# More repeated identity passes while TensorE waits for the last weights

## Chip, cores, metric

One core of a Trainium2 chip. The metric is the device time of one execution in microseconds (us); medians are quoted with their ranges. A profiled execution's span, from its first to its last recorded event, is some 1.8 us shorter than its time. "Clock" is the share of full speed that the throttle granted TensorE.

## The reference, cut to what matters

Sparse causal attention (8 batches, 8 heads, 576 positions, 64 per head) feeds a spectral mix. Each of the 64 lowest frequencies m is multiplied by its own complex 512 x 512 weights; those weights are nearly all of the data read.

```python
X = np.fft.rfft(x, axis=1)
Xr, Xi = (np.real(X[:, :n_modes]), np.imag(X[:, :n_modes]))
Yr = np.einsum('bmd,mde->bme', Xr, w_r) - np.einsum('bmd,mde->bme', Xi, w_i)
Yi = np.einsum('bmd,mde->bme', Xr, w_i) + np.einsum('bmd,mde->bme', Xi, w_r)
Y[:, :n_modes] = Yr + 1j * Yi
y = np.fft.irfft(Y, n=S, axis=1)
u = x + y
return (u + np.maximum(u @ w_ch, 0.0)).astype(np.float32)
```

## The kernel before

The weights come in two halves of 64 modes each. `mode` is 16 matmuls of 16 columns. After mode 53 of the second half TensorE has little left to do until weights land, and the kernel issues `again`: matmuls of 512 columns with the identity matrix, whose result nobody reads ("passes" below), to keep TensorE's clock up for what follows. Modes 60 to 63 have loads of their own; earlier modes share one in pairs.

```python
def mode(slot, m):
    ...                                   # cut: w_fetch, bank choice
    for e in range(4):
        for c in range(4):
            nc.tensor.matmul(yv[:, mi, e, :], wt[pr, XC[c], ds(128 * e, 128)],
                             Xh[half][pr, c, :, :, m],
                             start=(c == 0), stop=(c == 3))
    ...                                   # cut: after modes 61 and 63 VectorE adds into YT

def again(n):
    for i in range(n):
        nc.tensor.matmul(warm, idn, v0s[0][:, 2, :], start=True, stop=True)

warm = psum("v")
for m in range(END, NM):                  # 54 .. 63
    mode(1, m)
    if m < END + 2:
        for w in early[3 * (m - END) : 3 * (m - END) + 3]:
            w()                           # five matmuls of the output stage
    else:
        again(0 if m < NM - 6 else 4 if m < NM - 2 else 2)
spec_last(0)                              # four products, four transposes of YT
again(3)
v_early(2, warm)
spec_out(3, 0, *held[0])                  # ScalarE, VectorE: copies to zz and yy
for i in range(len(units)):               # output stage, 36 tiles
    v_rows(i)                             # cut; starts with a matmul on zz
    ...
```

The softmax here doesn't subtract the row's maximum and nothing guards it: scores larger than these inputs give would overflow.

## Time and profile before

| | kernel before |
|---|---|
| time, three runs | 434.84 us median (434.26 to 434.90) |
| profiled execution | span 433.8 us, so a time of 435.61 us |
| busy share PE, VectorE, ScalarE | 78%, 50%, 43% |
| chain that ended last | DMA 69%, PE 18% |
| granted clock, mean | 0.833 |

In TensorE's timelines L547 is `mode`, L951 `again`, L886 and L884 the last spectra, and L688 with v<-zz the first work of the output stage.

### The profile page before, as it was taken

To read this page: it belongs to the slowest core of one execution; us is meant where nothing else is said; L and a number is where in the kernel's file an instruction comes from. 1 tells how busy PE (TensorE), PEld (TensorE's weight loads), DVE (VectorE), ACT (ScalarE), POOL (GpSimd) and SP (SyncE) were. 2 spreads that over 40 slices of the span, in tenths; PEclk is the share of its full clock that TensorE was granted. 3 is DMA by queue.
4 is the path that set the end of the run, shared out by engine and by line. 5 is a ranking of instruction groups with operands and counts; after the bars stand their busy time and mean duration, and the time that the engine had idled before them with its cause. 6 is when DMAs were issued, how large, how long until landed. Compare 5 with 4: busy or idle time off the path is not lost.

```text
span 433.8 us, 12099 instructions
## 1 busy us (share of the span) xinstructions
PE 338.7 (78%) x5307; PEld 244.0 (56%) x5307; DVE 215.1 (50%) x466; ACT 188.1 (43%) x353; POOL 128.9 (30%) x208
## 2 busy tenths in 40 slices
PE   1986888779886887889794566698669698977994
PEld 1865776657764665667663344465446465643441
DVE  2888678744523243342511033455346366503895
ACT  1686678635543435445340401133115122602892
POOL 6522332323232222222222222222222221200983
PEclk9999899869967659676855559868798899988999
DMA  8999999999999999999999999999999999991687
GB/s 178 212 213 213 215 212 212 212 210 213 215 212 214 213 214 213 213 214 214 213 213 213 213 213 215 213 213 215 213 213 213 214 213 213 214 179 29 260 331 275
DMA packets 28996, 92.18 MB, mean 212 GB/s; under 512 B 4048, under 2 KB 5072, under 8 KB 28944
## 3 DMA queue, kind: packets, MB, share of 16 engines
q0 software_dynamic: 24704, 81.28, 94.3%
q1 hardware_dynamic: 3440, 9.46, 5.8%
q10 hardware_dynamic: 800, 0.67, 0.6%
q8 instruction: 42, 0.69, 0.6%
q14 instruction: 10, 0.08, 0.0%
HBM read 163.22 MB, written 9.44 MB: 398 GB/s over the span
## 4 chain that ended last, share of the span: by engine, by line
DMA 69%; PE 18%; DVE 6%; ACT 3%; issue 2%; POOL 1%; DVEq 0%; POOLq 0%
DMA wt<-in_moe_w_i_dram 51%; DMA wt<-in_moe_w_r_dram 8%; DMA ring<-in_q_dram 5%; DMA w_ch<-in_moe_w_ch_dram 5%; DVE xb L250 2%; DVE kz L292 2%; PE y L547 2%; PE v L688 2%; PE u L688 2%; PE v L894 2%; PE sc L514 1%; ACT X L260 1%; DVE rec L249 1%; PE tp L395 1%; PE sc L353 1%
## 5 line engine op out<-in xcount | busy, mean ns | idle before, releaser
L547 PE MATMUL y<-X,wt 128*128 128x16 f16 (+1 forms) x2048 | 82.8, 192 | 59.5 <-DMA wt<-in_moe_w_i_dram 58.1
L547 PEld LDWEIGHTS <-wt 128*128 128x128 f16 (+1 forms) x2048 | 73.1, 103 | 75.4 <-issue 68.3
L196 POOL DMA_DIRECT2D wt<-in_moe_w_r_dram x62 | 36.4, 587 | 139.2 <-PE y L547 66.0
L196 POOL DMA_DIRECT2D wt<-in_moe_w_i_dram x60 | 35.2, 587 | 73.0 <-DMA wt<-in_moe_w_i_dram 60.2
L654 ACT ACTIVATE v<-sc 128x512 f16<-128x512 f32 x32 | 19.1, 596 | 68.4 <-PE sc L645 68.3
L471 ACT ACTIVATE PL<-sc 128x480 f16<-128x480 f32 (+1 forms) x48 | 27.7, 579 | 47.6 <-PE sc L457 46.9
L645 PE MATMUL sc<-w_cp,xT 128*128 128x512 f16 (+1 forms) x160 | 47.4, 424 | 0.0
L655 DVE COPY xo<-tp 128x512 f16<-128x512 f16 x32 | 22.1, 692 | 36.7 <-PE tp L653 36.4
L250 DVE TENSOR_TENSOR xb<-av,rec 90x256 f16<-90x256 f32 (+2 forms) x80 | 36.0, 450 | 2.8
L249 DVE RECIPROCAL rec<-av 90x4 f32<-90x4 f32 (+2 forms) x80 | 14.7, 183 | 45.3 <-PE av L486 33.9
L402 DVE COPY qT<-tp 128x576 f16<-128x576 f16 x16 | 12.0, 758 | 40.1 <-PE tp L395 37.2
L260 ACT ACTIVATE v<-tp 128x640 f16<-128x640 f16 (+1 forms) x24 | 19.4, 807 | 24.0 <-PE tp L429 21.1
L395 PE MATMUL tp<-cI_s,ring 64*64 64x64 f16 x864 | 26.4, 211 | 1.6 <-issue 0.8
L360 ACT ACTIVATE PL<-sc 90x360 f16<-90x360 f32 (+1 forms) x48 | 22.7, 490 | 6.2 <-PE sc L353 5.3
L926 DVE TENSOR_TENSOR osb<-u,rl 128x512 f32<-128x512 f32 x36 | 23.6, 689 | 3.3 <-ACT rl L907 1.7
L395 PEld LDWEIGHTS <-ring 64*64 64x64 f16 x864 | 20.7, 123 | 6.8 <-issue 3.6
L441 PE MATMUL sc<-cMl_s,cI_s 128*128 128x480 f16 (+1 forms) x48 | 23.0, 478 | 1.6 <-ACT X L260 1.6
L909 POOL TENSOR_TENSOR rl<-rl,xo 128x512 f32<-128x512 f32 x16 | 18.3, 1155 | 18.9 <-ACT rl L907 18.6
L457 PE MATMUL sc<-qT,kz 128*128 128x160 f16 (+1 forms) x160 | 23.4, 275 | 0.5 <-issue 0.5
L457 PEld LDWEIGHTS <-kz 128*128 128x128 f16 x160 | 16.8, 119 | 10.8 <-issue 8.1
L907 ACT ACTIVATE rl<-v 128x512 f32<-128x512 f32 x36 | 20.4, 597 | 4.9 <-PE v L688 4.2
L285 PE MATMUL tp<-cI_s,ring 72*128 72x72 f16 x256 | 15.1, 206 | 9.5 <-DMA ring<-in_v_dram 8.0
(103 smaller groups left out, 655.5 us busy)
## 6 DMA issues: line engine op xcount, KB each, us to landing
wt<-in_moe_w_r_dram POOLq DMA_DIRECT2D x62, 512.0 KB, 18.9
wt<-in_moe_w_i_dram POOLq DMA_DIRECT2D x60, 512.0 KB, 19.4
out_dram<-osb SPq DMA_DIRECT2D x14, 512.0 KB, 2.7
ring<-in_v_dram POOLq DMA_DIRECT2D x8, 288.0 KB, 13.4
ring<-in_q_dram POOLq DMA_DIRECT2D x8, 288.0 KB, 13.6
ring<-in_k_dram POOLq DMA_DIRECT2D x8, 288.0 KB, 13.0
ring<-in_v_dram POOLq DMA_DIRECT2D x3, 512.0 KB, 15.1
ring<-in_q_dram POOLq DMA_DIRECT2D x3, 512.0 KB, 14.8
```

Of the source, the lines that this page charges most:

```text
L196: nc.gpsimd.dma_start(dst, rows)
L250: nc.vector.tensor_tensor(out=dst, in0=val.rearrange("p h (q c) -> p h c q", c=4), in1=rec[0:n, 0:pieces] .to_broadcast((n, pieces, 64)) . ...
L260: nc.scalar.activation(out=out, in_=in_, func=ACTF.Copy)
L360: nc.scalar.activation(out=PS[0:n, ds(POFF[t], 4 * n)], in_=scp[0:n, 0 : 4 * n], func=ACTF.Exp, scale=SCALE,)
L395: nc.tensor.transpose(tp[ds(64 * hp, 64), ds(64 * i, 64)], qn[ds(64 * hp, 64), ds(64 * (9 * g + i), 64)], idn[ds(64 * hp, 64), ds(64 * hp, ...
L441: nc.tensor.matmul(scp[:, 0 : n * times].rearrange("p (h x) -> p h x", h=times), idn, mask_rows("cMl", n, times), start=True, stop=False,)
L457: nc.tensor.matmul(scp[:, ds(col, n)], kzs[par][:, hp, ds(s0, 128)], qTs[par][:, ds(s0, n)], start=False, stop=(i == len(todo) - 1),)
L471: nc.scalar.activation(out=dst, in_=src, func=ACTF.Exp, scale=SCALE)
L547: nc.tensor.matmul(yv[:, mi, e, :], wt[pr, XC[c], ds(128 * e, 128)], Xh[half][pr, c, :, :, m], start=(c == 0), stop=(c == 3),)
L645: nc.tensor.matmul(vp[pr, :], xT[:, ch, cols], w_chs["cp"][:, ch, :], start=(ch == 0), stop=(ch == 3),)
L655: nc.vector.tensor_copy(out=xo[pr].rearrange("p (h q c) -> p h q c", h=2, c=4), in_=tp[pr, 0:512].rearrange("p (h c q) -> p h q c", h=2, c=4),
L926: nc.vector.tensor_tensor(out=osb[:, t % 2, :], in0=up, in1=rls[b, t][:, t % 2, :], op=AluOp.add)
```

## The change

Intent: hold TensorE at full clock through the last spectra. The number of passes before mode 62 rises from 16 to 24, and three instead of two stand before mode 63.

```diff
-            again(0 if m < NM - 6 else 4 if m < NM - 2 else 2)
+            again({NM - 1: 2, NM - 2: 3, NM - 3: 10}.get(m, 7 if m > NM - 6 else 0))
```

| passes after mode | 58 | 59 | 60 | 61 | 62 | 63 | sum |
|---|---|---|---|---|---|---|---|
| before | 4 | 4 | 4 | 4 | 2 | 2 | 20 |
| changed | 0 | 7 | 7 | 10 | 3 | 2 | 29 |

## The prediction

> **What bounds the kernel now.** I read the page first. Its chain that ended last is 69% DMA, most of it weights, and its line of granted clock shows TensorE below full speed in many slices. So until the last weights land the kernel runs at the pace of their transfer, and what TensorE does before then counts only if it makes TensorE late for them. Next I read the chain of waits piece by piece for the stretch in which the diff acts; columns are start, length, what.
>
> ```profile
> 364.40 19.38 DMA wt<-in_moe_w_i_dram
> ...
> 384.06 9.63 DMA wt<-in_moe_w_i_dram
> 393.83 0.64 PE y L547 x16
> 394.47 0.50 PE v L951 x2
> 394.97 1.77 PE y L886 x4
> 396.74 0.43 PE y L884 x4
> 397.17 1.18 PE v L951 x3
> 398.35 0.22 PE v L894
> 398.56 0.23 PE v L688
> ```
>
> From 384.06 to 393.69 the chain is a transfer, so the idle passes (L951) before it are off the path. From 393.83 TensorE's own pace is the path: mode 63, two passes, the four products and four transposes of the last spectra (L886, L884), three more passes, an early v, then the output stage. The same four L886 matmuls take 0.86 us later in this chain, at 408.68, against 1.77 here: the clock is at half speed here. The timeline of TensorE shows the sequence ahead of it:
>
> ```profile
> 383.92 0.64 PE L547 MATMUL y<-X,wt 128*128 128x16 f16 x16 [2.88 <-DMA wt<-in_moe_w_i_dram]
> 384.39 1.83 PE L951 MATMUL v<-v,cI_s 128*128 128x512 f16 x4
> 386.02 0.68 PE L547 MATMUL y<-X,wt 128*128 128x16 f16 x16
> 386.54 1.67 PE L951 MATMUL v<-v,cI_s 128*128 128x512 f16 x4
> 388.04 0.64 PE L547 MATMUL y<-X,wt 128*128 128x16 f16 x16
> 388.52 1.02 PE L951 MATMUL v<-v,cI_s 128*128 128x512 f16 x4
> 389.38 0.64 PE L547 MATMUL y<-X,wt 128*128 128x16 f16 x16
> 389.86 1.03 PE L951 MATMUL v<-v,cI_s 128*128 128x512 f16 x4
> 392.58 0.64 PE L547 MATMUL y<-X,wt 128*128 128x16 f16 x16 [1.69 <-DMA wt<-in_moe_w_i_dram]
> 393.83 0.64 PE L547 MATMUL y<-X,wt 128*128 128x16 f16 x16 [0.17 <-DMA wt<-in_moe_w_i_dram]
> ```
>
> These are modes 58 to 63 with their passes. Modes 62 and 63 wait for weights (1.69 and 0.17 us idle); 60 and 61 do not. The stretch table in half microseconds gives the clock (the last column but two):
>
> ```profile
> 387.50:388.00 0.50, 0.50 (x3) 0.15 (x1) 0.00 (x0) 0.00 (x0) 0.00 (x0) 0.63 0.54 107
> 394.50:395.00 0.50, 0.50 (x3) 0.13 (x2) 0.29 (x1) 0.00 (x0) 0.00 (x0) 0.70 0.00 0
> 398.00:398.50 0.50, 0.50 (x4) 0.20 (x2) 0.38 (x1) 0.00 (x0) 0.00 (x0) 0.89 0.00 0
> ```
>
> The clock is 0.50 between such rows and 1.00 outside. A mean of 0.70 is 0.30 us at full and 0.20 at half speed, so the changes fall at 394.70 (to half) and 398.11 (back), and likewise at 387.87 (back) and 384.46 (to half, from a row with 0.96).
>
> **What the Trainium skill says.** (1) "TensorE: Matmul & The Clock Gate", Part 1: the clock is full or half, decided by a free-running activity window of 3413 ns that does not restart with the kernel. The trace agrees: the four changes lie 3.41, 6.83 and 3.41 us apart, one, two and one windows. (2) The same page, "Back-to-back issue gap": N/1.2 ns cold and N/2.4 + 2.5 warm, 427 and 216 ns for 512 columns. In the trace four passes at full clock fill 388.52 to 389.38, 0.215 us each; at half clock the first four fill 384.39 to 386.02, 0.41 each with the seam. (3) The same page, "HAM oscillation", says a gap over some 3.4 us costs the clock. The trace is stricter: an idle of 1.69 us was enough, as the rest of that window held mostly 16-column matmuls.
>
> I therefore counted matmul columns per window on that grid, from the groups by form. For the window 391.29 to 394.70:
>
> ```profile
> L547 PE MATMUL y<-X,wt 128*128 128x16 f16 x32 | 1.3, 192 | 1.9 <-DMA wt<-in_moe_w_i_dram 1.9
> L951 PE MATMUL v<-v,cI_s 128*128 128x512 f16 x4 | 1.3, 396 | 0.0
> ```
>
> 32 x 16 + 4 x 512 = 2560 columns, and the next window is at half clock. Over 250 to 430 us, full-clock windows with up to 2880 columns were followed by half clock, those with 3392 or more by full. I take some 3200 as the border, an estimate.
>
> **The change, part by part.** It removes the four passes after mode 58 and adds three after each of 59 and 60, six after 61, one after 62: 20 becomes 29, none after 63 changed. The instruction order shows only that on TensorE; the streams of VectorE, ScalarE and GpSimd are the same. No transfer moves: the last weight load issues at 384.06, waiting only for earlier transfers, and the first altered TensorE instruction comes at 384.39. Weights of 62 and 63 thus again permit starts at 392.58 and 393.83.
>
> Replay with the grid as traced, 0.48 us per mode:
> - Mode 59 at 384.39 to 384.86; seven passes at half clock, 7 x 0.427 = 2.99, to 387.85, just at the boundary.
> - Mode 60 to 388.33; seven at full, 7 x 0.216 = 1.51, to 389.84; mode 61 to 390.32 (its weights were in by 389.38); ten, 2.16, to 392.48. That ends 0.10 before mode 62 may start: nothing is late, and the idle of 1.69 is filled.
> - Mode 62 to 393.06; three, 0.65, to 393.71; mode 63 at 393.83 as before; two passes.
> - Window 391.29 to 394.70 now holds 5.5 passes (2816) + 256 + 1536 + 256 + about 950 = 5,800 columns. The clock stays full at 394.70.
> - L886 starts at 394.85 as before, since VectorE's add for mode 63 ends at 394.50 + 0.29. Then 4 x 0.216 = 0.86, transposes 0.22, three passes 0.65, the early v 0.22: 396.80. The copies of zz need L886's end, 395.88, plus 0.04, ScalarE 0.37, a seam 0.03, VectorE 0.42: 396.74, so they do not hold it. The first zz matmul starts at 396.80 where it started at 398.40.
>
> The gain is **1.60 us**. It should reach the end whole: from 401 on TensorE runs with hardly a gap at clock 1.00 to its last matmul at 427.3, and all behind it shifts. 434.84 - 1.60 = 433.24 us, 0.37%.
>
> **Rivals.** *A: the grid lies elsewhere, and the passes come in the way.* It is free-running, so another execution may have its boundaries elsewhere. Say at 383.0, 386.4, 389.83: the idle of 2.88 us takes the clock down at 383.0, and the window to 386.4 holds two modes and 3.6 passes, 2,360 columns, so it stays half to 389.83. Then: seven passes to 387.85, mode 60 to 388.33, 3.5 cold to 389.83, 3.5 warm to 390.59, mode 61 to 391.07, ten to 393.23. Mode 62 is 0.65 late and ends at 393.71; with three passes mode 63 begins at 394.36, **0.53 us late**. The kernel before, with 8 fewer passes up to mode 62, is in time there: its passes end at 391.4, and its last windows hold some 3,460 columns, above the border, so its last spectra run at full clock too. It would then take 433.2 and the changed kernel 433.8. Going round the grid by this arithmetic, about a third of positions gain 1.4 to 1.7, a sixth change nothing, half lose 0 to 0.8; the mean is -0.35 us. Against A: the profiled execution sits in the good third, and the three times before lie within 0.64 us, less than the two states of the kernel before would differ.
>
> *B: the gain is lost in the output stage.* The last 10 us write at 352 GB/s with DMA share 0.93 to 0.96, so the output transfers might be the bound. Then an earlier start of TensorE is worth less: 434.3 to 434.8. Against it: the chain runs through TensorE to 426.8, not through transfers, and the first output too is made earlier.
>
> *C: the copies or the relus take over.* ScalarE's relus and zz copies from 398.81 to 401.18 are on the chain; if one is fixed by something other than TensorE, part of 1.60 is lost, perhaps 0.3 us. Nothing in the waits points to it.
>
> **Range and chances.** I give the traced grid (-1.6) and a random one (-0.35) equal weight: -0.97, so 433.9 us. The low end 433.0 is the whole gain with 0.2 of scatter; the high end 435.3 is a bad grid position in rival A. A change of 2% would be 8.7 us, five times the largest gain and ten times the largest loss worked out: faster 0.005, same 0.985, slower 0.01.
>
> **What would show it right or wrong.** Right: mode 62 starts with about 0.1 us of idle, not 1.69; four L886 take 0.86 at clock 1.00 between 394 and 398; the first zz matmul comes about 1.6 us sooner against the last weights' landing. Rival A: mode 62 starts with no wait for DMA, after its weights have landed, and clock 0.50 reaches beyond 388. Rival B: new gaps of TensorE after 401, or a longer way from the last matmul to the end. It is wrong altogether if the last landing itself moves by over 1 us.

## The result, and the profile after

| | before | changed |
|---|---|---|
| median of 6 runs | 434.63 us (433.93 to 435.04) | 435.12 us (434.19 to 435.32) |
| ratio, changed over before | | 1.0009 (95% interval 0.9996 to 1.0022) |
| profiled span | 433.8 us | 433.3 us |

Ratios here and below are the mean time of one kernel's fast runs over that of the other's of the same rounds, so not quite the ratio of the medians. The trace shows the last spectra at full clock, as predicted. This is the chain of waits of the changed kernel in the same stretch (start, length, what):

```profile
385.76 2.93 PE v L951 x7
...
391.16 2.16 PE v L951 x10
393.32 0.63 PE y L547 x16
393.95 0.65 PE v L951 x3
394.60 0.59 PE y L547 x16
395.19 0.43 PE v L951 x2
395.62 0.99 PE y L886 x4
396.62 0.22 PE y L884 x4
396.84 0.65 PE v L951 x3
```

The products L886 take 0.99 us where they took 1.77, the transposes 0.22 instead of 0.43, the three passes 0.65 instead of 1.18. The stretch table (clock in the last column but two) has the fall and the return of the clock early, and 1.00 during the last spectra:

```profile
385.50:386.00 0.50, 0.50 (x11) 0.27 (x8) 0.00 (x0) 0.00 (x0) 0.00 (x0) 0.70 0.82 164
389.00:389.50 0.50, 0.50 (x8) 0.21 (x5) 0.00 (x0) 0.00 (x0) 0.00 (x0) 0.89 0.55 107
396.00:396.50 0.50, 0.50 (x4) 0.24 (x3) 0.00 (x0) 0.00 (x0) 0.00 (x0) 1.00 0.00 0
```

To compare executions, I count time from the start of mode 58, which waits for its weights in every trace. From there to the first zz matmul it is 398.40 - 383.92 = 14.48 us before and 397.54 - 384.64 = 12.90 us after: **1.58 us less**, where 1.60 was predicted. From the first zz matmul to TensorE's last it is 28.90 us in both. The span shows only 0.5 us, because mode 58 began 0.72 us later and the way from TensorE's last matmul to the end took 0.4 us longer. The late start has nothing to do with the change. In the timeline of GpSimd, which issues the loads, most of that lag is there at 25 us, where both kernels' instructions are identical. The kernel before, then the changed one:

```profile
24.56 0.58 POOL L227 DMA_DIRECT2D ring<-in_v_dram  x1 [2.90 <-PE tp L269]
```

```profile
25.18 0.58 POOL L227 DMA_DIRECT2D ring<-in_v_dram  x1 [1.58 <-PE tp L269]
```

So a difference of 1.58 us lies in one pair of traces, and none in the times of six runs each. Where is it? And is it the change that made it? The two traces differ in one more thing: the clock fell to half 0.54 us after mode 58 began in the first and 1.06 us in the second.

### The profile page after: what moved, and what is told of

Its sections match the earlier page's. It is cut to its first block, busy times and chain, and to the rows that moved or that the text cites. A ratio compares the mean times of both kernels' runs of the same rounds, so it can differ in the third digit from the quotient of the medians.

```text
span 433.3 us, 12117 instructions
## 1 busy us (share of the span) xinstructions
PE 336.6 (78%) x5316; PEld 242.4 (56%) x5316; DVE 215.3 (50%) x466; ACT 187.8 (43%) x353; POOL 128.9 (30%) x208
## 4 chain that ended last, share of the span: by engine, by line
DMA 82%; PE 12%; issue 2%; DVE 1%; ACT 1%; POOL 1%; DVEq 0%; POOLq 0%
DMA wt<-in_moe_w_i_dram 55%; DMA ring<-in_v_dram 8%; DMA ring<-in_k_dram 6%; DMA w_ch<-in_moe_w_ch_dram 5%; DMA wt<-in_moe_w_r_dram 4%; DMA ring<-in_q_dram 4%; PE v L951 2%; PE u L688 2%; PE v L688 2%; PE v L894 2%; PE y L547 1%; PE u L915 1%; PE tp L324 1%; PE tp L285 1%; DVE kz L292 0%
## 5 line engine op out<-in xcount | busy, mean ns | idle before, releaser
L645 PE MATMUL sc<-w_cp,xT 128*128 128x512 f16 (+1 forms) x160 | 48.7, 433 | 0.0
L260 ACT ACTIVATE kz<-tp 64x360 f16<-64x360 f16 (+1 forms) x32 | 19.0, 593 | 11.6 <-PE tp L395 10.1
L441 PE MATMUL sc<-cMl_s,cI_s 128*128 128x480 f16 (+1 forms) x48 | 21.8, 454 | 1.6 <-ACT X L260 1.6
L457 PE MATMUL sc<-qT,kz 128*128 128x160 f16 (+1 forms) x160 | 22.3, 265 | 0.2 <-issue 0.2
```

The costliest lines, as they stand in the source:

```text
L260: nc.scalar.activation(out=out, in_=in_, func=ACTF.Copy)
L441: nc.tensor.matmul(scp[:, 0 : n * times].rearrange("p (h x) -> p h x", h=times), idn, mask_rows("cMl", n, times), start=True, stop=False,)
L457: nc.tensor.matmul(scp[:, ds(col, n)], kzs[par][:, hp, ds(s0, 128)], qTs[par][:, ds(s0, n)], start=False, stop=(i == len(todo) - 1),)
L645: nc.tensor.matmul(vp[pr, :], xT[:, ch, cols], w_chs["cp"][:, ch, :], start=(ch == 0), stop=(ch == 3),)
```

## The experiments

**Theory 1, the grid.** The clock is decided in windows of 3.41 us whose grid lies elsewhere in each execution. The kernel before pays the 1.58 us only on some positions; its profiled execution was one of them. The changed kernel pays this on none, but on others its passes stand in front of weights that have landed.
**Theory 2.** The gain is there in every execution and is lost elsewhere: in later weights, or in output transfers that set the end.

Twelve runs came in three calls of four; those of one call share a chip and the runs of the kernel before (11 per call). All gave correct results. I first give them one by one, then the traces in one table.

### e1 and e8: the kernel before, again

No edit.

> The kernel before, unchanged, for a second trace and for the noise. Theory 1 (grid): the position of the 3.41 us clock grid against the last weights changes from execution to execution, so the clock changes will lie elsewhere than 0.54 us after mode 58's first matmul; the first zz matmul comes 12.9 us after mode 58 starts if the clock is full through the last spectra and 14.4 to 14.5 if it is at half there. Theory 2 (the gain is real in every execution and is lost elsewhere: in later weights or in the output transfers): the grid lies as before, 14.5 us again. Time: ratio 1.000 within 0.15% by both.

Measured: 434.90 us median, ratio 0.9998 (0.9977 to 1.0019); six of its own runs spread from 434.10 to 436.41. The trace is not as the first. TensorE's timeline:

```profile
384.19 0.64 PE L547 MATMUL y<-X,wt 128*128 128x16 f16 x16 [2.88 <-DMA wt<-in_moe_w_i_dram]
392.82 0.64 PE L547 MATMUL y<-X,wt 128*128 128x16 f16 x16 [0.88 <-DMA wt<-in_moe_w_i_dram]
395.13 1.04 PE L886 MATMUL y<-w_ch,YT 128*128 128x512 f16 x4
397.09 0.81 PE L688 MATMUL v<-zz,cA_s 128*128 128x512 f16 x3
```

The same program, and the four L886 matmuls take 1.04 us instead of 1.89; the first zz matmul is 397.09 - 384.19 = 12.90 us after mode 58. The clock was at half from 383.34 to 390.17, two windows. So the passes before mode 62 ran slower and ended later, the wait for mode 62 was 0.88 us instead of 1.69, and the window with it held enough work to keep the clock. This execution of the kernel *before* already has all that the change can give.

> The kernel before, a third trace. Theory 1: first zz matmul 14.3 to 14.5 us after mode 58 if a clock change falls 3.1 to 3.41 or 0 to 0.9 us after mode 58's start (modulo 3.41), and 12.9 otherwise, in step with the mean clock at the four L886 matmuls (0.86 us or 1.77 us).

Measured: one run, 436.43 us, beside 435.55 us median. Its timeline:

```profile
384.53 0.64 PE L547 MATMUL y<-X,wt 128*128 128x16 f16 x16 [2.88 <-DMA wt<-in_moe_w_i_dram]
395.72 1.91 PE L886 MATMUL y<-w_ch,YT 128*128 128x512 f16 x4
398.83 0.81 PE L688 MATMUL v<-zz,cA_s 128*128 128x512 f16 x3
```

Here L886 is slow again, and the first zz matmul comes 14.30 us after mode 58. The clock fell at 384.41, 0.12 us before mode 58, which is 3.29 modulo 3.41: in the range that theory 1 had named. Theory 2 as put (the grid as in the first trace) is out.

### e2, e9, e12: the changed kernel, again

No edit.

> The changed kernel again. Theory 1: in about half of the positions the passes end after the weights of mode 62 have landed; the first zz matmul then comes 12.9 to 13.7 us after mode 58's start, and the time against the kernel before is between -0.1 and +0.1%. Theory 2: 12.9 us in this trace too, with time the same.

Measured: 434.86 us median, ratio 0.9992 (0.9976 to 1.0009); first zz matmul 12.91 us after mode 58.

> The changed kernel a third time, to be set against the filled one on one chip, and to catch a bad grid. Theory 1: if the clock changes to half 1.5 to 3.1 us after mode 58 starts (modulo 3.41), mode 62 starts without a wait 8.7 to 9.5 us after mode 58 and the first zz matmul comes 13.0 to 13.7 us after it, otherwise 12.9. Time between -0.2 and +0.1% against the kernel before. A trace at 14.3 or more would go against theory 1.

Measured: 434.12 us median (433.82 to 434.77), ratio 0.9975 (0.9958 to 0.9992), a little outside the expected -0.2%. First zz matmul 12.93 us after mode 58, on a grid at 1.66.

> The changed kernel a fourth time, one look for another grid position: 12.9 us, or 13.0 to 13.7 if the clock change falls 1.5 to 3.1 us after mode 58's start (modulo 3.41).

Measured: one run, 433.67 us; 12.89 us on a grid at 1.45.

Four traces of the changed kernel give 12.89 to 12.93; none has the 14.3 or more of the kernel before. None caught the worst grids for it, at 2 to 3.1, either. And there is a larger gap: all four lie at 1.06 to 1.66, outside the positions on which theory 1 lets the kernel before lose (0 to 0.9 and 3.1 to 3.41). So no trace shows the changed kernel where the kernel before loses its clock. That it keeps it there is argued from the columns in its windows and not shown, and by theory 1 the 1.58 us between the first two traces come from their grids: on the second one the kernel before would have had 12.9 us too.

### e3: no passes at all

```diff
-            again(0 if m < NM - 6 else 4 if m < NM - 2 else 2)
+            again({}.get(m, 0))
```

> All idle passes between modes 58 and 63 left out (the three after the last spectra stay). No window then holds 3200 columns, so the clock is at half when the last spectra begin, in every execution, whatever the grid. Theory 1: first zz matmul 14.3 to 14.6 us after mode 58's start, and time +0.25 to +0.5% (+1.1 to +2.2 us) over the kernel before, which pays this only in some executions. Theory 2 with the output transfers as the bound: later first zz matmul, but the time within 0.1% of the kernel before.

Measured: 435.74 us median (435.14 to 436.13), ratio 1.0010 (0.9991 to 1.0028). The trace is as theory 1 has it: half clock from 385.42 to 399.1, first zz matmul 399.18 - 384.54 = 14.64 us after mode 58. The time is below the expected +0.25%, though its interval reaches 0.28%; the mean difference of 0.46 us was to be 1.3 by the arithmetic below. This run also shows the landings, since nothing stands in front of the modes:

```profile
388.21 0.64 PE L547 MATMUL y<-X,wt 128*128 128x16 f16 x16 [2.56 <-DMA wt<-in_moe_w_i_dram]
389.47 0.64 PE L547 MATMUL y<-X,wt 128*128 128x16 f16 x16 [0.62 <-DMA wt<-in_moe_w_i_dram]
393.17 0.64 PE L547 MATMUL y<-X,wt 128*128 128x16 f16 x16 [3.06 <-DMA wt<-in_moe_w_i_dram]
394.43 0.64 PE L547 MATMUL y<-X,wt 128*128 128x16 f16 x16 [0.62 <-DMA wt<-in_moe_w_i_dram]
```

Modes 60 to 63 may start 3.67, 4.93, 8.63 and 9.89 us after mode 58. In all traces where mode 62 waits, it starts at 8.62 to 8.67.

### e4: passes after mode 57 too

Passes are given as mode: number in this and the next diffs.

```diff
-59: 7, 60: 7, 61: 10, 62: 3, 63: 2
+57: 10, 59: 7, 60: 7, 61: 14, 62: 3, 63: 2
```

> As the change, and ten passes more after mode 57 (in the idle of 2.88 us before mode 58) and fourteen instead of ten after mode 61. The clock should then never fall from 377 on, so the number of passes that fits is known: at full clock they end about 0.7 us before mode 62's weights. Theory 1: clock 1.00 from 380 to the end in every position of the grid, mode 62 waits 0.3 to 1 us for weights, first zz matmul 12.9 us after mode 58, time below both kernels: -0.1 to -0.25% against the kernel before. Theory 2: the same 12.9 us and no gain in time.

Measured: 434.83 us median, ratio 0.9986 (0.9967 to 1.0005), in the expected range but not clear of noise. The clock is 1.00 from 376 to the end, as expected. But the passes did not end before mode 62's weights: mode 62 starts 9.15 us after mode 58, 0.5 late, and the first zz matmul comes at 13.27. My count had taken mode 60's weights to be in; it waited 1.03 us for them, to 3.67 after mode 58, and everything behind slid.

### e5: ten passes too many

```diff
-59: 7, 60: 7, 61: 10, 62: 3, 63: 2
+59: 7, 60: 7, 61: 20, 62: 3, 63: 2
```

> As the change, but twenty passes after mode 61 instead of ten: passes in front of landed weights, on purpose. From the traces so far mode 62's weights land 8.63 to 8.66 us after mode 58 starts. Theory 1 (passes after the landing cost their full time, up to the end): mode 62 starts 10.4 to 11.6 us after mode 58 without a wait, first zz matmul 14.5 us after mode 58 on a good grid and up to 15.8 on a bad one, time +0.2 to +0.6% against the kernel before. Theory 2 (lost in the output): the same start of the output stage, time within 0.1%.

Measured: 436.81 us median (436.44 to 437.05), ratio 1.0029 (1.0006 to 1.0052). Timeline:

```profile
384.33 1.12 PE L547 MATMUL y<-X,wt 128*128 128x16 f16 x32 [2.88 <-DMA wt<-in_moe_w_i_dram]
391.25 4.48 PE L951 MATMUL v<-v,cI_s 128*128 128x512 f16 x20
395.57 0.64 PE L547 MATMUL y<-X,wt 128*128 128x16 f16 x16
399.63 0.81 PE L688 MATMUL v<-zz,cA_s 128*128 128x512 f16 x3
```

Mode 62 starts 11.24 us after mode 58, 2.6 after its weights, with no wait; the first zz matmul comes at 15.30, 2.40 us later than the best, and TensorE's last matmul 28.90 after that, as ever. Passes in front of landed weights cost their time up to TensorE's last matmul, and the ratio of the times is clear of 1. The trace also shows a bad grid (half clock from 383.10 to 389.93) for the part that this kernel shares with the changed one: mode 61 ends and the passes begin at 391.25. With ten of them, 2.16 us, mode 62 would start at 393.41, 0.43 after its weights; with three more, mode 63 at 394.5, 0.3 late. That is rival A of the prediction, measured up to mode 61 and worked out from there.

### e6 and e10: passes fitted to the landings

```diff
-59: 7, 60: 7, 61: 10, 62: 3, 63: 2
+57: 11, 59: 10, 60: 3, 61: 13, 62: 3, 63: 2
```

> Passes fitted to the landings that the runs so far show (mode 60 3.67, 61 4.93, 62 8.63, 63 9.89 us after mode 58): eleven after mode 57, ten after 59, three after 60, thirteen after 61, three and two after 62 and 63, 42 in all. Theory 1: clock 1.00 from 380 on, each of modes 58, 60, 61, 62, 63 waits 0.1 to 0.7 us for its weights, first zz matmul 12.9 us after mode 58 on every grid; against the kernel before, which I work out at 13.4 on average over the grid, -0.5 us or -0.1%, against the changed kernel -0.05%. Theory 2: 12.9 and no difference in time.

Measured: 434.74 us median (434.08 to 434.89), ratio 0.9979 (0.9960 to 0.9998). Timeline:

```profile
384.27 1.12 PE L547 MATMUL y<-X,wt 128*128 128x16 f16 x32 [0.50 <-DMA wt<-in_moe_w_i_dram]
387.97 0.64 PE L547 MATMUL y<-X,wt 128*128 128x16 f16 x16 [0.42 <-DMA wt<-in_moe_w_i_dram]
392.93 0.64 PE L547 MATMUL y<-X,wt 128*128 128x16 f16 x16 [0.25 <-DMA wt<-in_moe_w_i_dram]
397.17 0.81 PE L688 MATMUL v<-zz,cA_s 128*128 128x512 f16 x3
```

Each of modes 58, 60 and 62 waits a little; 61 and 63 start 4.96 and 9.92 us after mode 58, within 0.03 of e3. The clock is 1.00 throughout, the first zz matmul comes at 12.90.

> The filled kernel again: clock 1.00 from 380 on, first zz matmul 12.9 us after mode 58; time 0.05 to 0.2% below the kernel before and 0 to 0.1% below the changed one, and the scatter of its times smaller than that of the kernel before. Theory 2: as both, within 0.05%.

Measured: 434.57 us median (433.94 to 435.24), ratio 0.9986 (0.9966 to 1.0005); clock 1.00 again, 12.90 us again. On the same chip the changed kernel (e9) took 434.12, so the expected advantage over it did not show. The scatter is smaller than that of the kernel before: standard deviations 0.31 and 0.53 us against 0.86 and 0.75.

### e7 and e11: each part of the change alone

```diff
-58: 4, 59: 4, 60: 4, 61: 4, 62: 2, 63: 2
+58: 4, 59: 4, 60: 4, 61: 10, 62: 3, 63: 2
```

> One part of the change alone: four passes stay after 58, 59 and 60, ten after 61 and three after 62. Theory 1: this part alone fills the idle before mode 62; the clock is full through the last spectra on every grid, and on a bad grid mode 62 is late by at most 0.4 us, since three passes fewer stand before it. First zz matmul 12.9 to 13.2 us after mode 58; time as the changed kernel or 0.03% below. Theory 2: no difference in time either.

Measured: 434.91 us median (434.62 to 435.29), ratio 0.9986 (0.9965 to 1.0006). The grid was a bad one (half clock to 390.37); mode 62 was 0.2 us late, and the first zz matmul at 12.97, within the expected range. This is the grid of e1 (2.55 and 2.56), where the kernel before had 12.90: here the added passes cost 0.07 us and gain nothing.

```diff
-58: 4, 59: 4, 60: 4, 61: 4, 62: 2, 63: 2
+59: 7, 60: 7, 61: 4, 62: 2, 63: 2
```

> The other part of the change alone: seven passes after 59 and 60, four after 61, two after 62. Theory 1: it does not fill the idle before mode 62, so it behaves as the kernel before: 14.3 to 14.5 us from mode 58 to the first zz matmul on a third of the grid positions (clock change 3.1 to 3.41 or 0 to 0.9 us after mode 58), 12.9 on the others, never late for mode 62. One look.

Measured: one run, 433.74 us; grid at 2.82, where no loss is expected, and 12.90 us; mode 62 waits 0.31 us. It agrees, but on this grid it separates nothing.

### All traces together

"Grid" is the fall of the clock to half, from mode 58's start, modulo 3.41. All in us.

| trace | grid | mode 62 starts after 58 | first zz matmul after 58 | last matmul after that | end of span after that |
|---|---|---|---|---|---|
| before | 0.54 | 8.66, waits | 14.48 | 28.90 | 6.5 |
| e8 before | 3.29 | 8.67, waits | 14.30 | 28.90 | 7.0 |
| e1 before | 2.56 | 8.63, waits | 12.90 | 28.91 | 6.2 |
| changed | 1.06 | 8.67 | 12.90 | 28.90 | 6.9 |
| e2 changed | 1.19 | 8.67 | 12.91 | 28.90 | 6.5 |
| e12 changed | 1.45 | 8.77 | 12.89 | 28.90 | 6.2 |
| e9 changed | 1.66 | 8.82 | 12.93 | 28.91 | 6.5 |
| e3 none | 0.88 | 8.63, waits | 14.64 | 28.90 | 5.9 |
| e4 after 57, too many | none | 9.15 | 13.27 | 28.90 | 6.7 |
| e5 ten too many | 2.18 | 11.24 | 15.30 | 28.90 | 6.5 |
| e6, e10 fitted | none | 8.66, 8.65, wait | 12.90 | 28.90 | 6.9, 6.6 |
| e7 after 61 only | 2.55 | 8.86 | 12.97 | 28.91 | 6.9 |
| e11 early only | 2.82 | 8.62, waits | 12.90 | 28.90 | 6.4 |

The fifth column refutes the second half of theory 2: the output stage does not give the gain back; it lasts 28.90 us whatever its start. The last column scatters by 1.1 us, with no clear relation to the fourth. Mode 58's own start scatters from 383.74 to 384.65 us over these traces. Those two are the noise that a gain of 1.58 on some executions must be seen through.

## Why the prediction was right or wrong

**The range held**: 435.12 us lies in 433.0 to 435.3, and "same" had 0.985. The central 433.9 was 1.2 us too low, and the first comparison gave +0.09% where I had expected a small gain. The top of the range had been set for a bad grid. No run shows that these six executions met bad grids, so that the range held there is partly luck.

**Replay: right in its terms, but tested on another grid.** 1.60 us predicted, 1.58 found, in each term of the last stretch: four L886 in about 0.86 per the next start (0.99 in the chain with its seam), transposes 0.22, three passes 0.65. Mode 62 was to start 0.10 us after the passes ended; it started as they ended, at the landing. The replay was for a clock that falls 0.54 us after mode 58; the trace had 1.06 and full clock only from 389.11, not 387.87. So the sizes were right, while the claim that the added passes save them on the first grid was not put to the test.

**No transfer moves: right.** The weights of modes 60, 62 and 63 land 3.52 to 3.59, 8.48 to 8.55 and 9.73 to 9.79 us after mode 58 starts in all fourteen traces; the modes can start some 0.13 us after that.

**The column count: right as a rule, misread at its border.** (A mode's matmul counts 16 columns, a pass 512.) The prediction's own listing refutes "those with 3392 or more by full": the windows from 275.23 and 305.95 us list 3392 columns each, and half clock follows both. The listing takes in matmuls that lie partly outside a window. Counting of each matmul only the part inside, over 250 to 425 us of all fourteen traces (703 windows), half clock followed every window of up to 3,070 columns and full clock every one of 3,257 or more; of the 18 between, 6 were followed by half clock. So 3200 was a good estimate. Counted so, the window with the wait for mode 62 held 2,475 columns in the first trace and 1,408 in e8, which lost the clock, and 3,853 in e1, which kept it.

**Rival B: wrong**, by the last two columns. **Rival C: wrong**: the zz matmul followed TensorE's own order and the rest came along whole.

**Rival A: right in that the grid moves, and the weight I gave it was the failing step.** "I give the traced grid (-1.6) and a random one (-0.35) equal weight." Nothing supported that half. The Trainium skill's "TensorE: Matmul & The Clock Gate", Part 1, says that the window is free-running, I quoted it, and still let one profiled execution count as much as all positions together. I argued from "the three times before lie within 0.64 us"; but the profiled execution itself, 435.61 us, stood 0.71 above the slowest of those three, and pointed to its being a slow draw. e1 and e8 settle it: of three traces of the kernel before, two have the loss and one does not. The rival's other half, passes that come in the way, was seen in the changed kernel for at most 0.17 us (mode 62 in e9).

With the random grid alone I would have said -0.35. Repeating the arithmetic with the landings of e3 for positions all round the grid gives a mean of 13.38 us from mode 58 to the first zz matmul before and 13.04 after, -0.34 us; this is an estimate. A second working of it gives 13.41 and 13.09, and meets the measured first zz matmul within 0.1 us in every trace. The three comparisons of times give mean differences of +0.41, -0.32 and -1.14 us. Their mean, -0.35, agrees, but the first and the third differ by more than their intervals, so the times alone do not settle even the sign. What stays open is how often each kernel meets each position: three and four traces are too few to say. And no trace caught the changed kernel where the kernel before loses, or on its own worst grids, where the arithmetic has its first zz matmul 0.3 to 0.8 us late.

**A version to prefer?** The fitted passes of e6 remove the grid from the question: they ran 0.21% and 0.14% below the kernel before, in one of two cases clear of noise, with less scatter. They were not shown faster than the changed kernel.

## What to carry to other kernels

Before crediting a change with removing a loss that one trace shows, ask whether that loss is there in every execution: compare the profiled execution's time with the timed ones, and take a second trace of the unchanged kernel. Before reading a gain from a pair of traces, see that both fell on the same kind of grid. Filler work that keeps a clock up should be fitted to the landing of each transfer and start early enough that the clock never falls; then its length is known, whereas filler that begins at an unknown clock lasts between one and two times its length at full clock (0.215 to 0.43 us a pass here) and may stand in front of the work it serves. A gain that only some executions have may show as less scatter, but that is a weak sign: e2, e6, e7, e9 and e10 scattered less than the kernel before, while the first six runs of the changed kernel (standard deviation 0.43 us) and e4 (0.70 us) scattered as much as it.

## What the Trainium skill lacked or had wrong

- "TensorE: Matmul & The Clock Gate", "Why this matters for your kernels", advises no TensorE gaps over some 3 us. In the kernel before, a gap of 1.69 us cost the clock, while 0.88 us (e1) did not. What told the two apart was how many columns the whole window held: in all fourteen traces up to 3,070 lost the clock and 3,257 or more kept it, whether the window itself ran at full or at half clock. Columns tell it better than busy time: the best single border in columns misplaces 5 of 703 windows, in busy time 59. The page names no such measure.
- The same page, Part 4, says that full clock does not engage for transposes, which do not count as busy in the same way. Here four 128-column transposes (`nc.tensor.transpose`, MATMUL in the trace) took 0.43 us at half clock and 0.22 at full, and transposes counted: without their columns the best single border misplaces 45 windows instead of 5. That transposes alone would bring full clock, no run shows.
- The same page calls the warm-up's cost under 1% of a span and run-variable. That agrees: 1.58 us of 434 is 0.36%. It lacks the consequence seen here: the same program has two durations of its tail (12.90 and 14.30 to 14.48 us in three traces), so one trace each cannot compare two kernels in it.
